# Attention feeding an activation product on one core: products of the first two slots interleaved, a bias moved ahead, and v's first load split

## The chip, the cores and the metric

The kernel runs on one core of one Trainium2 chip. The metric is the device time of one execution in microseconds; the time before the change is 308.69 us, the median of three runs (308.67 to 309.40). The profile is one execution of 308.5 us, of which the program's own instructions span 306.7 us.

## The reference

Two parts follow one another. First, attention in a sliding window of 32 to each side, for 8 batches of 8 heads with 576 positions of 64 values. Then the result of each batch, laid out as 576 rows of 512 values (4,608 rows in all), goes through two matrix products with a smoothed ReLU between them.

```python
scores = np.where(np.abs(pos[:, None] - pos[None, :]) <= 32, q @ k.T / 8, -1e9)
x = softmax(scores) @ v                 # 8 batches x 8 heads x 576 x 64 -> 4608 x 512
h = x @ w_in                            # 512 -> 2048
g = np.where(h >= 1, h, np.where(h <= -1, 0.0, (h + 1) ** 2 / 4))
out = g @ w_out                         # 2048 -> 512
```

All inputs and the output are 32-bit floats. The kernel computes in bf16 with 32-bit sums; its loads from memory convert while they run.

## The kernel before, in words

**Slots.** The second part is cut into slots. Slot `a` is block `t` of 256 rows of x (18 blocks) and piece `f` of 256 columns of w_in (8 pieces), `t, f = divmod(a, 8)`, in the loop at L482. A slot does eight TensorE products (L504: two column halves `j`, four pieces `kk` of the 512 inputs), a Relu on ScalarE (L508), and either a maximum and a product on VectorE (L515, L516) or, in the seven slots named at L379, a Square on ScalarE (L512) and one VectorE step (L513). The result stands in gT. Products with w_out follow slots later: L460 by pairs for the first two blocks (list at L378), L444 afterwards. The sum of a slot stands in one of two PSUM buffers of the pool ps_h; only slot 6 borrows one of ps_o. So slot 9 uses the buffer of slot 7, slot 10 that of slot 8.

**Attention.** It is spread among the slots by a table written out by hand (L394 to L413): scores (L227) with a band bias added by TensorE first (L206, in `add_mask`) as long as `a < 14`, Exp on ScalarE (L235), the sums with v and with ones (L293), Ln and Exp for the reciprocal (L299, L300), and a VectorE product that writes x, turned, into xT (L305). xT has four pieces `kk` of two heads each, written two at a time: one call makes pieces `y` and `y + 2`. The sums of `y = 0` fill pieces 0 and 2, those of `y = 1` pieces 1 and 3.

**The start.** Before the slots, q and k of the first half of batch 0 are turned on TensorE (L189, L187) and copied out (L190, by ScalarE and VectorE), their scores made, and the first 256 rows of x (L365 and L367, ended by L369 and L370). `keep_warm(n, ...)` puts n products of no use (L336) where TensorE would wait. Slot 1 then turns the second half of q and k (L394), and slot 2 makes the scores that need it.

**The loads.** All engines work in the order of the program (L73). GpSimd issues the loads of L85 (halves of q and k), L106 (v), L110 (w_in), L115 (w_out), L92 and L98 (q and k of later batches) in one queue. Its order at the start is: k's first half; four pieces of v for batch 0; w_in's columns 0 to 511 as four loads (256 columns, two halves of the partitions each); the second halves of q and k; w_in's columns 512 to 1023 as four loads, 1024 to 1535 as two, 1536 to 1791 as two; w_out; the last columns of w_in. Then GpSimd copies the masks (L151, L153) and goes on with w_out and the next batches. Each of these loads waits until the one issued eight before it has landed, as the semaphores of the built program show. v of a batch stands in `vn` as 18 chunks of 64 positions by two heads; chunks 0 to 8 belong to `y = 0`, 9 to 17 to `y = 1`. The first 256 rows of x need chunks 0 to 4 and 9 to 13; the sums of slot 3 need chunks 5 to 7 beside, and those of slots 4 and 5 need the rest.

Of the kernel before, what the change touches and what calls it, by code (L numbers as in the profile page):

```python
# [7 lines left out]
FP = mybir.dt.float32  # L8
# [6 lines left out]
def kernel(  # L15
# [84 lines left out]

    def load_v(b, n):
        if b not in vn:
            vn[b] = nat.tile([128, 2 * NC, 2, D], BF, name="vn", tag="vn", bufs=3)
        h, a = divmod(n, 2)
        y = NY * h + 2 * a
        nc.gpsimd.dma_start(out=vn[b][64 * a:64 * a + 64, :, h], in_=v[b, y:y + 2].rearrange("y s d -> (y s) d")  # L106
                            .rearrange("(c r) d -> r c d", r=64))

# [24 lines left out]
    for n in range(4):  # L133
        load_v(0, n)
    V.memset(ones, 1.0)
# [6 lines left out]
    def put(todo):  # L142
        for fn, *x in todo:
            fn(*x)
# [3 lines left out]
    w += [(load_w_in, c, c + 256, h) for c in range(1536, DFF, 256) for h in range(2)]  # L148
    put(w[:4] + [(load_half, 1, t, h) for t in range(2) for h in range(2)] + w[4:12])
    put([(load_w_out, 0, 0, 4)] + w[12:])  # L150
# [59 lines left out]

    def scores(b, ys, pars, cs, eng, pool=ps_s, w=128):

        if b not in pt:
            pt[b] = ptp.tile([128, 2, 2, 2, 512], BF, name="pt")
        ps = two_banks(pool)
        n = 0
        if eng is None:
            cols = (ys[1] - ys[0]) * (pars[1] - pars[0]) * (cs[1] - cs[0])
            add_mask([ps[:, h] for h in range(2)], cols, w)
# [126 lines left out]
    with tc.tile_pool(name="ps_p", bufs=1, space=bass.MemoryType.PSUM) as ps_p:  # L346
        keep_warm(11, ps_h, "hp")

        V.memset(qkT(0, 0).rearrange("d (y s) -> d y s", y=NY)[:, :, S // 2:352], 0.0)
        for b in range(LONG):  # L350
            V.memset(qkT(b, 0).rearrange("d (y s) -> d y s", y=NY)[:, :, S - PAD:], 0.0)
        V.memset(qkT(0, 1).rearrange("d (y s) -> d y s", y=NY)[:, :, S // 2:320], 0.0)
        qn[0, 0] = cast(q32, "qb", 5)
        qq = [tpose(0, n, 0, (A.copy, V.tensor_copy)[n], tp1(ps_h)) for n in range(2)]
        for x in qq:
            x()
        kk = [tpose(0, n, 1, (A.copy, V.tensor_copy)[n], tp1((ps_n, ps_p)[n])) for n in range(2)]
        keep_warm(3, ps_h, "hp")
        for x in kk:
            x()  # L360
        scores(0, (0, 1), (0, 2), (0, 2), None)
        scores(0, (0, 2), (0, 1), (2, 3), None, ps_n, 32)
        scores(0, (1, 2), (0, 2), (0, 2), None, ps_p)
        keep_warm(4, ps_h, "hp")
        e0 = sums(0, 0, 0, TB)  # L365
        keep_warm(2, ps_h, "hp")
        e1 = sums(0, 1, 0, TB, ps_p)  # L367
        keep_warm(7, ps_h, "hp")
        e0()  # L369
        e1()  # L370
# [98 lines left out]
    def run(pos):  # L469
# [9 lines left out]
        for end in todo:  # L479
            end()  # L480

    for a in range(NF * NB + NF):  # L482
        t, f = divmod(a, NF)
# [10 lines left out]
        if t < NB:  # L494
            if t not in gT:
                gT[t] = gtp.tile([128, 2 * NF, TB], BF, name="gT", tag="gT")
            r0 = TB * t % RING
            if a == 6:
                hp = ps_o.tile([128, 2, TB], FP, name="hp", tag="op")
            else:  # L500
                hp = ps_h.tile([128, 2, TB], FP, name="hp", tag="hp")
            for j in range(2):
                for n, kk in enumerate((0, 2, 1, 3)):
                    nc.tensor.matmul(hp[:, j], w_in[:, kk, 256 * f + 128 * j:256 * f + 128 * j + 128],  # L504
                                     xT[:, kk, r0:r0 + TB], start=n == 0, stop=n == 3)

# [47 lines left out]
```

The softmax here doesn't subtract the row's maximum and nothing guards it: scores larger than these inputs give would overflow.

## Time and profile before

| What | us |
|---|---|
| median of three runs | 308.69 |
| span of the profile | 306.7 |
| PE busy | 299.9 (98%) |
| VectorE busy | 242.1 (79%) |
| ScalarE busy | 192.5 (63%) |
| products of the slots, L504, 1,152 | 149.4 |
| products with w_out, L444, 496 | 126.9 |
| first product of a slot | 13.73 |

The page gives busy times for each engine: PE is TensorE's matrix work, PEld its loads of weights, DVE VectorE, ACT ScalarE, POOL GpSimd, whose issue of loads counts as its work. Where it has 40 slices, each digit is a tenth of busy time in 1/40 of the span, some 7.7 us. A line of the timeline has a start in us, a length, an engine, a line of the code and an operation, and in brackets the idle time of the engine before it with what ended it. "Landing" is the time from the issue of a load until its data is announced. A start of the chain of waits is followed by the length and the work that the end of the program was waiting for.

### The profile page before, as it was taken

What the parts mean: (1) busy time and instruction counts of PE and PEld (TensorE: products, weight loads), DVE (VectorE), ACT (ScalarE), POOL (GpSimd) and SP (SyncE); (2) the same over time, 40 slices, a digit from 0 to 9 for tenths busy, and PEclk for the clock granted to TensorE, in tenths of its full rate; (3) what the DMA queues carried; (4) which work ended last, traced back from release to release, by engine and by line L of the source; (5) the groups of instructions that cost most, each with busy time, mean ns of one, the idle gap of its engine ahead of it and who ended that gap; (6) DMA issues with size and microseconds to landing.
All of it is one profiled execution on the core that took longest, in us unless ns stands there. A gap on an engine that the chain in (4) does not pass through costs nothing.

```text
span 306.7 us, 8496 instructions
## 1 busy us (share of the span) xinstructions
PE 299.9 (98%) x3650; PEld 206.6 (67%) x3650; DVE 242.1 (79%) x376; ACT 192.5 (63%) x320; POOL 77.4 (25%) x92
## 2 busy tenths in 40 slices
PE   8989999999999999999999999999999999999995
PEld 3567878876666666666666666666666666666654
DVE  4278568888888888889888888889888888888760
ACT  3688886738856767666656666566676666554431
POOL 8799461028008106400450003700000000000000
PEclk9999999999999999999999999999999999999999
DMA  9999999999999999996899156990811010010111
GB/s 153 182 197 198 177 201 152 174 152 149 138 206 89 170 191 107 159 94 142 102 170 138 34 108 91 167 150 17 177 50 36 34 36 36 35 36 34 60 45 68
DMA packets 137173, 35.70 MB, mean 116 GB/s; under 512 B 122160, under 2 KB 132912, under 8 KB 137136
## 3 DMA queue, kind: packets, MB, share of 16 engines
q0 software_dynamic: 102976, 18.06, 83.2%
q1 hardware_dynamic: 34016, 16.81, 25.6%
q8 instruction: 28, 0.46, 0.6%
q10 hardware_dynamic: 144, 0.29, 0.3%
q14 instruction: 9, 0.07, 0.1%
HBM read 36.70 MB, written 9.44 MB: 150 GB/s over the span
## 4 chain that ended last, share of the span: by engine, by line
PE 89%; ACT 3%; DVE 2%; DMA 2%; issue 1%; POOL 1%; POOLq 0%; ACTq 0%
PE hp L504 39%; PE op L444 36%; PE bb L293 6%; PE op L460 4%; PE bb L227 2%; DMA vn<-in_v_dram 2%; PE op L433 1%; ACT pt L235 1%; POOL vn L106 1%; PE tp L187 1%; DVE xT L305 1%; ACT rc L300 1%; DVE mx L515 1%; ACT lr L299 1%; DVE gT L513 0%
## 5 line engine op out<-in xcount | busy, mean ns | idle before, releaser
L504 PE MATMUL hp<-xT,w_in 128*128 128x256 bf16 x1152 | 149.4, 273 | 1.7 <-DMA w_in<-in_moe_w_in_dram 0.8
L508 ACT ACTIVATE rr<-hp 128x512 f32<-128x512 f32 x144 | 85.7, 595 | 87.8 <-PE hp L504 87.7
L504 PEld LDWEIGHTS <-w_in 128*128 128x128 bf16 x1152 | 112.0, 98 | 41.1 <-issue 2.3
L444 PE MATMUL op<-w_out,gT 128*128 128x512 bf16 x496 | 126.9, 380 | 0.0
L515 DVE TENSOR_TENSOR mx<-hp,rr 128x512 f32<-128x512 f32 x137 | 94.5, 690 | 30.8 <-ACT rr L508 28.9
L516 DVE SCALAR_TENSOR_TENSOR gT<-rr,mx 128x512 bf16<-128x512 f32 x137 | 95.2, 695 | 4.7
L444 PEld LDWEIGHTS <-gT 128*128 128x128 bf16 x496 | 46.1, 98 | 34.8
L98 POOL DMA_DIRECT2D qn<-in_q_dram x12 | 14.6, 1221 | 111.4 <-DMA kT<-kn 107.5
L235 ACT ACTIVATE pt<-bb 128x1024 bf16<-128x1024 f32 (+1 forms) x33 | 32.7, 1002 | 5.0 <-PE bb L227 3.7
L305 DVE TENSOR_TENSOR xT<-bb,rc 128x512 bf16<-128x512 f32 (+1 forms) x32 | 21.0, 658 | 10.1 <-ACT rc L300 9.6
L106 POOL DMA_DIRECT2D vn<-in_v_dram x32 | 27.5, 891 | 4.9 <-DMA w_out<-in_moe_w_out_dram 4.2
L300 ACT ACTIVATE rc<-lr 128x512 f32<-128x512 f32 (+2 forms) x40 | 23.5, 587 | 1.3
L449 ACT COPY osb<-op 128x512 f32<-128x512 f32 x31 | 18.1, 583 | 8.7 <-PE op L444 8.3
L299 ACT ACTIVATE lr<-bb 128x512 f32<-128x512 f32 (+2 forms) x40 | 22.0, 551 | 0.4 <-PE bb L293 0.3
L201 DVE TENSOR_TENSOR pt<-pt,mask 128x1024 bf16<-128x1024 bf16 (+1 forms) x33 | 20.3, 614 | 0.5 <-ACT pt L235 0.5
L293 PE MATMUL bb<-pt,ones 64*64 64x256 bf16 (+3 forms) x352 | 19.6, 256 | 0.1
L293 PE MATMUL bb<-pt,vn 64*64 64x128 bf16 (+3 forms) x712 | 18.4, 204 | 0.1
L293 PEld LDWEIGHTS <-vn 64*64 64x64 bf16 x712 | 16.7, 107 | 0.3 <-DMA vn<-in_v_dram 0.3
L460 PE MATMUL op<-w_out,gT 128*128 128x256 bf16 x128 | 16.5, 273 | 0.0
L293 PEld LDWEIGHTS <-ones 64*64 64x64 bf16 x352 | 10.2, 105 | 8.9 <-issue 8.9
L98 POOL DMA_DIRECT2D kn<-in_k_dram x12 | 14.6, 1230 | 0.5 <-issue 0.5
L227 PE MATMUL bb<-qT,kT 64*64 64x128 bf16 (+1 forms) x520 | 13.1, 217 | 0.3 <-DVE kT L190 0.2
(59 smaller groups left out, 115.1 us busy)
## 6 DMA issues: line engine op xcount, KB each, us to landing
out_dram<-osb SPq DMA_DIRECT2D x35, 256.0 KB, 2.5
vn<-in_v_dram POOLq DMA_DIRECT2D x32, 144.0 KB, 10.2
qn<-in_q_dram POOLq DMA_DIRECT2D x12, 288.0 KB, 6.9
kn<-in_k_dram POOLq DMA_DIRECT2D x12, 288.0 KB, 8.9
w_in<-in_moe_w_in_dram POOLq DMA_DIRECT2D x12, 128.0 KB, 5.7
w_out<-in_moe_w_out_dram POOLq DMA_DIRECT2D x4, 256.0 KB, 6.6
w_out<-in_moe_w_out_dram POOLq DMA_DIRECT2D x2, 512.0 KB, 15.8
kh<-in_k_dram POOLq DMA_DIRECT2D x4, 144.0 KB, 5.1
```

Of the source, the lines that this page charges most:

```text
L98: nc.gpsimd.dma_start(out=x[:, :, h], in_=src[b, NY * h:NY * h + NY].rearrange("y s d -> (y s) d") .rearrange("(u p) d -> p u d", p=128))
L106: nc.gpsimd.dma_start(out=vn[b][64 * a:64 * a + 64, :, h], in_=v[b, y:y + 2].rearrange("y s d -> (y s) d") .rearrange("(c r) d -> r c d", ...
L235: A.activation(p, ps[:, :, :w * n].rearrange(like, y=m), AF.Exp, scale=D ** -0.5)
L293: nc.tensor.matmul(bb[HD[h], a, o + c0:o + c1], ones[HD[a]] if c is None else vn[b][HD[a], c, h], p(a, h), start=n == 0, stop=True, skip_g ...
L299: A.activation(lr[:, :, :D0], bb[:, :, D0:2 * D0], AF.Ln)
L300: A.activation(rc[:, :, :D0], lr[:, :, :D0], AF.Exp, scale=-1.0)
L444: nc.tensor.matmul(o, gT[tt // 2][:, j, 128 * (tt % 2):128 * (tt % 2) + 128], w_out[:, j], start=not done, stop=len(done) == 2 * NF - 1, s ...
L460: nc.tensor.matmul(o[:, tt], gT[p][:, j, 128 * tt:128 * tt + 128], w_out[:, j, 256 * half:256 * half + 256], start=not done, stop=len(done ...
L504: nc.tensor.matmul(hp[:, j], w_in[:, kk, 256 * f + 128 * j:256 * f + 128 * j + 128], xT[:, kk, r0:r0 + TB], start=n == 0, stop=n == 3)
L508: A.activation(rr, hp, AF.Relu, scale=0.5, bias=0.5)
L515: V.tensor_max(mx, hp, rr)
L516: V.scalar_tensor_tensor(g, rr, 1.0, mx, op0=ALU.min, op1=ALU.mult)
```

## The change

Three things are changed at the start; what is computed stays the same.

v of batch 0 is loaded in two steps: chunks 0 to 13 of its four pieces where all 18 were loaded before, and chunks 14 to 17, again as four loads, behind w_in's columns 512 to 767. This is meant to bring v's first part, and the loads behind it, in earlier.

The bias of the first scores is added ahead of k's copies instead of after them, with one product of no use in front of it for three; further fillers are fewer (three for four, none for two, six for seven). This is meant to let the first scores begin as soon as k's copies end.

The products of slots 0 and 1 are interleaved: all eight that need the first half of x (pieces 0 and 2), for both slots, and then the eight that need the second half. This is meant to use the time between the two halves of x. The order of later slots stays as it is.

```diff
-    def load_v(b, n):
+    def load_v(b, n, c0=0, c1=2 * NC):
...
-        nc.gpsimd.dma_start(out=vn[b][64 * a:64 * a + 64, :, h], in_=v[b, y:y + 2].rearrange("y s d -> (y s) d")
-                            .rearrange("(c r) d -> r c d", r=64))
+        nc.gpsimd.dma_start(out=vn[b][64 * a:64 * a + 64, c0:c1, h], in_=v[b, y:y + 2].rearrange("y s d -> (y s) d")
+                            .rearrange("(c r) d -> r c d", r=64)[:, c0:c1])
...
-        load_v(0, n)
+        load_v(0, n, 0, 14)
...
-    put(w[:4] + [(load_half, 1, t, h) for t in range(2) for h in range(2)] + w[4:12])
+    put(w[:4] + [(load_half, 1, t, h) for t in range(2) for h in range(2)]
+        + w[4:6] + [(load_v, 0, n, 14, 2 * NC) for n in range(4)] + w[6:12])
...
-    def scores(b, ys, pars, cs, eng, pool=ps_s, w=128):
+    def scores(b, ys, pars, cs, eng, pool=ps_s, w=128, ready=None):
...
-        ps = two_banks(pool)
+        ps = ready or two_banks(pool)
         n = 0
-        if eng is None:
+        if eng is None and not ready:
...
-        keep_warm(3, ps_h, "hp")
+        keep_warm(1, ps_h, "hp")
+        first = two_banks(ps_s)
+        add_mask([first[:, h] for h in range(2)], 4, 128)
         for x in kk:
             x()
-        scores(0, (0, 1), (0, 2), (0, 2), None)
+        scores(0, (0, 1), (0, 2), (0, 2), None, ready=first)
         scores(0, (0, 2), (0, 1), (2, 3), None, ps_n, 32)
         scores(0, (1, 2), (0, 2), (0, 2), None, ps_p)
-        keep_warm(4, ps_h, "hp")
+        keep_warm(3, ps_h, "hp")
         e0 = sums(0, 0, 0, TB)
-        keep_warm(2, ps_h, "hp")
         e1 = sums(0, 1, 0, TB, ps_p)
-        keep_warm(7, ps_h, "hp")
+        keep_warm(6, ps_h, "hp")
...
+    def project(hp, f, r0, todo, first, last):
+
+        for n, (j, kk) in enumerate(todo):
+            nc.tensor.matmul(hp[:, j], w_in[:, kk, 256 * f + 128 * j:256 * f + 128 * j + 128],
+                             xT[:, kk, r0:r0 + TB], start=first and n == 0, stop=last and n == len(todo) - 1,
+                             skip_group_check=True)
...
-            r0 = TB * t % RING
-            if a == 6:
-                hp = ps_o.tile([128, 2, TB], FP, name="hp", tag="op")
-            else:
-                hp = ps_h.tile([128, 2, TB], FP, name="hp", tag="hp")
-            for j in range(2):
-                for n, kk in enumerate((0, 2, 1, 3)):
-                    nc.tensor.matmul(hp[:, j], w_in[:, kk, 256 * f + 128 * j:256 * f + 128 * j + 128],
-                                     xT[:, kk, r0:r0 + TB], start=n == 0, stop=n == 3)
+            if a == 0:
+                hps = [ps_h.tile([128, 2, TB], FP, name="hp", tag="hp") for _ in range(2)]
+                for y in range(2):
+                    for f2 in range(2):
+                        project(hps[f2], f2, 0, [(j, y + 2 * m) for j in range(2) for m in range(2)], y == 0, y == 1)
+            elif a > 1:
+                pool, tag = (ps_o, "op") if a == 6 else (ps_h, "hp")
+                hps = [pool.tile([128, 2, TB], FP, name="hp", tag=tag)]
+                project(hps[0], f, TB * t % RING, [(j, kk) for j in range(2) for kk in (0, 2, 1, 3)], True, True)
+            hp = hps.pop(0)
```

## The prediction

> **What bounds the kernel now.** I read the page's busy shares first, then the chain of waits for the start, then the timeline from 16 to 33 us with all engines, then the single lines that issue transfers. The page says where time can be won at all:
>
> ```profile
> PE 299.9 (98%) x3650; PEld 206.6 (67%) x3650; DVE 242.1 (79%) x376; ACT 192.5 (63%) x320; POOL 77.4 (25%) x92
> ...
> PE   8989999999999999999999999999999999999995
> ...
> DMA  9999999999999999996899156990811010010111
> ```
>
> TensorE is full but for the first slices, so only an earlier entry into the full stretch moves the end. Asked for PE's waits between 60 and 210 us, the trace names none. The chain of waits for the start reads (start, length, what):
>
> ```profile
> 5.50 5.13 DMA vn<-in_v_dram
> ...
> 10.67 0.52 PE bb L293 x17
> ...
> 11.22 0.61 ACT lr L299
> ...
> 13.80 0.70 DVE xT L305
> ...
> 14.54 1.70 PE hp L504 x14
> ...
> 18.93 0.65 DVE kT L190
> ```
>
> v's last piece lands at 10.63, the softmax sums follow, ScalarE does Ln and Exp twice, and the second half of x is ready at 14.50. From there the chain runs through slot 1's activation and the copies of k. This is the stretch that the change shortens. What comes next decides what the end gets of it. The timeline (start, length, engine, line, operation):
>
> ```profile
> 18.02 1.03 PE L504 MATMUL hp<-xT,w_in 128*128 128x256 bf16 x8 [0.59 <-DMA w_in<-in_moe_w_in_dram]
> ...
> 20.14 1.05 PE L504 MATMUL hp<-xT,w_in 128*128 128x256 bf16 x8
> ...
> 21.43 0.62 ACT L508 ACTIVATE rr<-hp 128x512 f32<-128x512 f32 x1
> ...
> 22.39 1.03 PE L504 MATMUL hp<-xT,w_in 128*128 128x256 bf16 x8 [0.24 <-DMA w_in<-in_moe_w_in_dram]
> ...
> 28.79 1.04 PE L504 MATMUL hp<-xT,w_in 128*128 128x256 bf16 x8
> ...
> 29.86 0.60 ACT L508 ACTIVATE rr<-hp 128x512 f32<-128x512 f32 x1 [0.48 <-PE hp L504]
> 30.30 1.03 PE L504 MATMUL hp<-xT,w_in 128*128 128x256 bf16 x8 [0.47 <-DVE gT L513]
> ...
> 31.15 0.69 DVE L513 SCALAR_TENSOR_TENSOR gT<-hp,mx 128x512 bf16<-128x512 f32 x1 [0.91 <-ACT mx L512]
> ...
> 32.04 1.04 PE L504 MATMUL hp<-xT,w_in 128*128 128x256 bf16 x8
> ```
>
> These are the products of slots 2, 3, 4, 8, 9 and 10. Slots 2 and 4 already wait for w_in, slot 4 for the 512-column pair. From slot 4's start at 22.39 to slot 8's end at 29.83 PE runs without a wait. So the chain through ScalarE and VectorE that ends in the 0.47 us wait at slot 9 has a second chain beside it, almost as long: transfer of w_in, slot 4, PE full. The transfers themselves, by the views of the lines that issue them: v's first four, then the 512-column w_in pair (min/median/max of an issue in ns, first and last start):
>
> ```profile
> L106 POOL DMA_DIRECT2D vn<-in_v_dram x4: 873/879/898, 2.9 to 5.5; - x4
> ...
> DMA to landing us min/median/max: 5.1/5.3/5.5
> ```
>
> ```profile
> L110 POOL DMA_DIRECT2D w_in<-in_moe_w_in_dram x2: 620/626/632, 15.2 to 15.8; - x2
> ...
> DMA to landing us min/median/max: 5.4/5.9/6.5
> ```
>
> The second of the pair is issued at 15.77 and lands 6.5 later, at 22.26: that is slot 4's wait.
>
> **What the Trainium skill says.** "DMA: Bandwidth & Descriptors", section "Issuing engines are not separate DMA queues": all queues share 16 engines. The trace agrees: the DMA view is full in every slice from 5 to 27 us, so moving bytes within a queue moves waiting from one consumer to the next and removes none. The same page, "Anatomy of one DMA", puts about 2 us of fixed cost on a transfer. Here a transfer issued into an idle queue at 67.13 or 92.90 shows its first packets after 1.9 us, and the loads above take 4.7 to 6.5, so most of that is queueing. "TensorE: Matmul & The Clock Gate", section "The HAM clock gate", lets the clock fall after an idle window of about 3.4 us; the page shows full clock throughout, and no gap that the change opens (below) reaches 0.5 us.
>
> **The change part by part.**
>
> *v cut to 14 of 18 chunks.* Each v piece is 147,456 bytes written, and the four drop 4/18 of that: 131,072 bytes. From 5.6 to 9.6 the DMA view moves 148 GB/s, so v's last piece lands 131,072 / 148,000 = 0.89 us earlier, at 9.75. The slot 0 and 1 sums of x need chunks 0 to 4 and 9 to 13 alone. All that is queued behind v gains the same 0.89: w_in's first four, the second half of q and k, w_in's third pair (slot 2's wait ends at 17.1).
>
> *Bias earlier, fewer warm-up products.* One warm-up of 0.21 in place of three lets the bias end before k's last copy ends at 8.15; the scores start at 8.19 for 8.37, so ScalarE's three Exp run from 8.63 to 10.74 for 8.81 to 10.92. The sums of the first half need the second Exp (9.83) and v (9.75), take the 0.67 that they took without their wait, and end at 10.5, behind the third Exp. Ln starts at 10.77 for 11.22: 0.45 won. Four ScalarE steps of 0.62 and one VectorE product of 0.70 follow unchanged: x's second half at 14.05 for 14.50. The dropped warm-ups leave PE gaps of 0.3 to 0.4; cost nil, since PE waits there anyway.
>
> *Products interleaved.* Eight products on the first half of x now run before 14.05 (12.8 to 13.7; w_in's second pair must land by then: 14.28 - 0.89 = 13.4). After the second half, slot 0 needs four products and slot 1 eight, where it was six and fourteen. At 1.70/14 = 0.121 each: slot 0 is done 0.45 + 2 x 0.121 = 0.7 earlier, slot 1 0.45 + 6 x 0.121 = 1.2 earlier. ScalarE takes slot 1's Relu at 15.3 for 16.27, its Square ends at 16.6 for 17.53; VectorE, with slot 0's two steps and slot 1's in front (16.03 becomes 15.3), ends the copy of k at 18.77 for 19.57. So the scores of slot 2 start **0.8 us** earlier. The transposes in front need k's second half, 16.70 - 0.89 = 15.8, in time.
>
> *The late chunks.* They are put between w_in's third and fourth pair. Bytes in front of the fourth pair and of the 512-column pair are then the same as before: their landings gain nothing. Four more transfers cost GpSimd 4 x 0.64 (the w_in row; by the v row at most 4 x 0.88), less 4 x 0.07 by which the shorter v issues shrink (0.88 for 18 chunks, 0.64 for w_in's 4, so 0.017 a chunk): some 2.3 us later issues. Each GpSimd load also waits for the eighth before it (0.28 after its landing, as the 1.1 us wait on that line shows for the load issued at 14.56), which is now a k half landing at 15.0 or 15.8: the fourth pair is issued at 15.3 and 16.1 for 12.83 and 14.56. Behind the waiting issues stand all later loads of w_in and w_out, for which slots 3 to 9 wait. The queue's backlog hides this if the first packets follow an issue by 1.9 us, as after the idle spells: 15.3 + 1.9 = 17.2, and the packets in front end at about 17.2. If a short load needs 3.0 (the first k load's 1.26 to its landing of 5.64, less 0.7 of issue and 0.7 of packets at 198 GB/s), the queue runs dry for up to 0.55. I take nil to 0.1, and keep 0.55.
>
> *The sum.* Slot 3's fourth pair lands at 19.3 as before, about when PE now wants it (20.14 - 0.8). Slot 4 would be reached at 21.4 but its pair lands at 22.3: PE's win is gone there but for the queue's +0.1. From slot 4 PE is full to slot 8's end, 29.83 + 0.1; the VectorE chain that made slot 9 wait until 30.30 is earlier now and no longer binds. Slot 8's Relu, Square and VectorE step still follow its products, 29.86 to 31.85, and free the buffer for slot 10: 31.9 + 0.1 for 32.04. The win at the end is 0.16 - 0.1 = **0.06 to 0.16 us** of the 0.8: 308.6.
>
> **The rivals.** *Carried through, 307.7 (33%).* If the 512-column pair lands earlier too, the win passes. For it: its second load needed 1.73 after the first, where 256 KB at 198 GB/s take 1.32, so 0.4 of that landing is a disturbance that may fall elsewhere; and the short transfers may overlap with their neighbours. Then slot 4 starts up to 0.8 to 1.0 earlier: 308.69 - 1.0 = 307.7. Against it: every byte in front of the pair is still there. *Queue dry, slower, 309.6 (25%).* A window of eight loads, four of them small, holds fewer bytes: 0.55 dry, the pair at 22.9, and w_out's second piece, issued 1.4 late (GpSimd's mask copies move along), lands at 28.4 to 28.7 where slot 7 wants it at 27.92. PE loses 0.55 at slot 4 and 0.4 there: 308.69 + 0.95 = 309.6. Against it: 1.9 us twice after idle spells. *Swallowed, 308.6 (42%)* is the forecast.
>
> **How the numbers follow.** Three quarters of the first rival lie below 307.76 (0.3% faster): 0.25. Seven tenths of the second lie above 309.62: 0.18. Within 0.3%: 0.57. The range reaches from under the first rival to the second, 307.5 to 309.6.
>
> **What would show it.** After: v's last landing near 9.75, Ln at 10.8, x's second half at 14.05, k's copy at 18.8; then slot 4's products waiting about 1 us for w_in and starting at 22.3 to 22.5, and slot 10's at about 31.9. The forecast is wrong if slot 4 starts before 22 (carried through), or if slot 3 or slot 7's w_out product waits long for its load (queue dry).

## The result, and the profile after

The changed kernel takes 312.72 us, the median of six runs (312.17 to 314.91), where the kernel before took 308.68 (six runs, 308.50 to 309.40). The ratio is 1.0142, with a 95% interval of 1.0108 to 1.0177: 4.0 us slower, outside the range that the prediction gave. A second comparison, with six more runs, gave 312.54 against 308.58, a ratio of 1.0136 (1.0114 to 1.0159). Ratios leave out runs over 1.5% above the fastest of the same kernel; these are one run of the kernel before, 440.26 us at a mean clock of 0.657, and one of the 17 runs of an experiment below, 314.18 us at 0.987.

The profiled execution spans 310.5 us, 3.8 more than before. The page of the changed kernel, its busy shares, three of its 40-slice rows and the group of the slots' products:

```profile
PE 294.3 (95%) x3607; PEld 206.9 (67%) x3644; DVE 241.8 (78%) x376; ACT 192.8 (62%) x320; POOL 79.5 (26%) x96
...
PE   7868999999999999999999999999999999999995
...
PEclk9997999999999999999999999999999999999999
...
GB/s 152 185 136 192 195 193 160 161 192 107 171 171 100 172 145 119 167 125 112 112 158 139 36 110 113 139 160 35 149 77 36 34 36 36 35 36 34 50 53 68
...
L487 PE MATMUL hp<-xT,w_in 128*128 128x256 bf16 x1152 | 150.6, 274 | 4.2 <-DMA w_in<-in_moe_w_in_dram 3.0
```

Two things are new. In the products' group, the waits that w_in's loads end sum to 3.0 us; they were 0.8 before. And the fourth digit of the clock is a 7: before, all were 9. All of it lies before 31 us; from slice 5 on, PE is as full as it was. The fall of PE's busy time from 299.9 is in part not real: 37 records of products are missing from this trace (3,607 for 3,644 weight loads), 35 of them in the w_out products of L446.

The timeline of PE in the changed kernel shows where it lies (start, length, engine, line, operation, and the idle time before it with what ended it):

```profile
17.97 1.03 PE L487 MATMUL hp<-xT,w_in 128*128 128x256 bf16 x8 [0.66 <-DVE gT L523]
...
20.64 1.03 PE L487 MATMUL hp<-xT,w_in 128*128 128x256 bf16 x8 [0.89 <-DMA w_in<-in_moe_w_in_dram]
...
24.75 1.70 PE L487 MATMUL hp<-xT,w_in 128*128 128x256 bf16 x8 [2.10 <-DMA w_in<-in_moe_w_in_dram]
...
27.30 1.56 PE L487 MATMUL hp<-xT,w_in 128*128 128x256 bf16 x8
...
34.06 1.03 PE L487 MATMUL hp<-xT,w_in 128*128 128x256 bf16 x8 [0.33 <-DVE gT L523]
...
35.81 1.03 PE L487 MATMUL hp<-xT,w_in 128*128 128x256 bf16 x8
```

These are slots 2, 3, 4, 5, 9 and 10. Slot 3 waits 0.89 us for w_in's fourth pair, slot 4 waits 2.10 for the 512-column pair. Slot 4 starts at 24.75 where it started at 22.39: 2.36 us later. Its eight products then take 1.70 in place of 1.03, slot 5's 1.56. Slot 10 starts at 35.81 for 32.04, 3.77 us later, and that is the whole difference of the spans (3.8). So the loss has two parts, **2.36 us at slot 4** and, since slot 9 waits 0.14 less than before, 3.77 - 2.36 + 0.14 = **1.55 us between slots 4 and 9**. The second part is the clock. The same trace cut into windows (from:to, length, then busy time and count of PE, PEld, DVE, ACT and POOL, the granted clock, the DMA share, and GB/s):

```profile
24.50:25.00 0.50, 0.25 (x3) 0.25 (x4) 0.50 (x1) 0.00 (x0) 0.50 (x2) 0.96 1.43 192
25.00:26.00 1.00, 1.00 (x7) 0.71 (x5) 0.01 (x1) 0.00 (x0) 1.00 (x2) 0.50 1.45 196
...
28.00:28.50 0.50, 0.50 (x5) 0.37 (x4) 0.50 (x1) 0.47 (x2) 0.50 (x1) 0.63 1.45 197
```

TensorE runs at half clock from about 24.96 (0.96 of the first window is 0.04 us at half) to about 28.37 (0.63 of the last is 0.37 us): 3.41 us, in which half of the work, 1.7 us, is lost. That is about the second part.

**What slot 4 waited for.** The chain of waits of the changed kernel's start (start, length, work):

```profile
6.10 2.36 POOL w_in L110 x4
8.47 6.03 DMA qh<-in_q_dram
...
14.78 1.22 POOL vn L106 x2
...
16.06 0.61 POOL w_in L110
...
16.86 1.22 POOL w_in L110 x2
18.08 0.04 issue
18.11 6.50 DMA w_in<-in_moe_w_in_dram
24.61 0.14 issue
24.75 1.70 PE hp L487 x8
```

Before, this chain ran over v, ScalarE and the products of slots 0 and 1. Now it runs through GpSimd's queue: a load of q that lands at 14.49, the third late piece of v that waited for its place, three w_in loads one after the other, and the transfer of the second half of the 512-column pair, issued at 18.11 for 15.77 and landing at 24.61 for 22.26. From issue to landing it took 6.50 us, as before (6.49), so here the delay could be put down to the issue alone. The run with the split alone (below) speaks against that: there the same load was issued 1.53 us later than before and took 7.32, and landed at 24.62. The windows show what happened to the transfers meanwhile. Before:

```profile
16.00:18.00 2.00, 1.44 (x39) 1.12 (x37) 1.82 (x3) 1.70 (x3) 2.00 (x4) 1.00 1.45 194
18.00:20.00 2.00, 1.75 (x38) 1.19 (x40) 1.84 (x4) 1.42 (x3) 1.90 (x4) 1.00 1.27 202
20.00:22.00 2.00, 2.00 (x72) 1.56 (x60) 1.55 (x2) 1.91 (x5) 2.00 (x3) 1.00 1.35 199
22.00:24.00 2.00, 1.76 (x53) 1.31 (x42) 1.38 (x2) 1.97 (x5) 2.00 (x3) 1.00 1.45 192
```

After:

```profile
16.00:18.00 2.00, 1.03 (x29) 0.73 (x24) 1.97 (x4) 1.97 (x4) 1.75 (x3) 1.00 1.34 114
18.00:20.00 2.00, 1.75 (x40) 1.21 (x40) 1.45 (x3) 1.22 (x3) 1.96 (x5) 1.00 1.10 125
20.00:22.00 2.00, 1.36 (x24) 1.01 (x28) 1.05 (x2) 1.33 (x4) 1.96 (x4) 1.00 1.10 148
22.00:24.00 2.00, 0.65 (x48) 0.51 (x36) 1.47 (x2) 1.97 (x4) 1.94 (x3) 1.00 1.21 157
```

The last column falls from 192 to 202 GB/s to 114 to 157 for 8 us. In these 8 us the queue moved 2 x (114 + 125 + 148 + 157) = 1,088 KB for 2 x (194 + 202 + 199 + 192) = 1,574 KB; the 486 KB that are missing are 2.5 us of transfer at 197 GB/s. That is slot 4's 2.36. The page's DMA row of tenths is full in both kernels and shows none of this: it says that the engines had a transfer, not how fast they moved it. The GB/s row does show it: its third slice is 136, and was 197 before.

### The profile page after: what moved, and what is told of

Its sections match the earlier page's. It is cut to its first block, busy times and chain, and to the rows that moved or that the text cites. A ratio compares the mean times of both kernels' runs of the same rounds, so it can differ in the third digit from the quotient of the medians.

```text
span 310.5 us, 8452 instructions
## 1 busy us (share of the span) xinstructions
PE 294.3 (95%) x3607; PEld 206.9 (67%) x3644; DVE 241.8 (78%) x376; ACT 192.8 (62%) x320; POOL 79.5 (26%) x96
## 4 chain that ended last, share of the span: by engine, by line
PE 88%; DMA 4%; POOL 3%; issue 2%; ACT 1%; DVE 0%; POOLq 0%; ACTq 0%
PE hp L487 39%; PE op L446 34%; PE bb L294 6%; PE op L462 4%; DMA w_in<-in_moe_w_in_dram 2%; PE bb L228 2%; DMA qh<-in_q_dram 2%; POOL vn L106 1%; POOL w_in L110 1%; PE op L435 1%; PE tp L188 1%; ACT pt L236 1%; POOL kh L85 0%; DVE gT L523 0%; ACT mx L522 0%
## 5 line engine op out<-in xcount | busy, mean ns | idle before, releaser
L446 PE MATMUL op<-w_out,gT 128*128 128x512 bf16 x461 | 119.6, 379 | 5.0 <-issue 4.8
L446 PEld LDWEIGHTS <-gT 128*128 128x128 bf16 x496 | 46.1, 98 | 34.8
L106 POOL DMA_DIRECT2D vn<-in_v_dram x36 | 29.7, 860 | 4.8 <-DMA w_out<-in_moe_w_out_dram 3.3
```

What stands on the lines that cost most here:

```text
L106: nc.gpsimd.dma_start(out=vn[b][64 * a:64 * a + 64, c0:c1, h], in_=v[b, y:y + 2].rearrange("y s d -> (y s) d") .rearrange("(c r) d -> r c ...
L446: nc.tensor.matmul(o, gT[tt // 2][:, j, 128 * (tt % 2):128 * (tt % 2) + 128], w_out[:, j], start=not done, stop=len(done) == 2 * NF - 1, s ...
```

## The experiments

The runs come in four groups, each beside runs of the kernel before: its median was 308.82 us beside the first four, then 308.79, 308.72 and 308.58. The theory that the expectations call Q is this. GpSimd's queue holds eight loads, since each waits for the landing of the one eight before it. A late load of v (chunks 14 to 17 of one piece, 32 KB) takes one of these eight places, and an issue of 0.61 us, as long as a load of w_in does, but brings a quarter of its bytes. With four of them in the queue there are too few bytes under way to keep the 16 DMA engines at their rate, and everything behind them comes later. The rivals are stated with each run. Where the expectations below say that "the fourth pair" lands at 22 us or later, the 512-column pair is meant; the fourth pair itself landed at 19.25 before and at 20.51 after.

### Which of the changes costs the time

The changed kernel with v's loads whole; the bias and the interleaved products stay:

```diff
-        load_v(0, n, 0, 14)
+        load_v(0, n)
...
-        + w[4:6] + [(load_v, 0, n, 14, 2 * NC) for n in range(4)] + w[6:12])
+        + w[4:12])
```

> The changed kernel with v's first load whole again (no late chunks): the early bias, the fewer fillers and the interleaved products stay. Theory Q (the four late loads hold back w_in, and the idle wait at slot 4 halves TensorE's clock): the loss goes; 308.3 to 308.7, the 512-column pair of w_in lands at 22.3, clock 1.00. Theory F (the dropped fillers or the new order of the products let the clock fall): the loss stays, over 311, with a stretch at half clock.

And the reverse, the kernel before with only the loads changed:

```diff
-        load_v(0, n)
+        load_v(0, n, 0, 14)
...
-    put(w[:4] + [(load_half, 1, t, h) for t in range(2) for h in range(2)] + w[4:12])
+    put(w[:4] + [(load_half, 1, t, h) for t in range(2) for h in range(2)]
+        + w[4:6] + [(load_v, 0, n, 14, 2 * NC) for n in range(4)] + w[6:12])
```

> The kernel before with v's load split alone, the late chunks behind w_in's third pair; bias, fillers and products as before. Theory Q: all of the loss is here, 312 to 313, the 512-column pair lands at about 24.6 and slot 4 waits for it by about 2 us. Theory F: 308.7, as before.

Without the split: 308.65 us, ratio 0.9993 (0.9979 to 1.0007). The bias and the interleaving alone move nothing that can be measured. The trace of that run holds a warning: its loads are those of the kernel before, yet the pair landed at 23.09 and slot 4 started at 23.23, both 0.8 us later than before (that execution took 309.22 us). So two single traces can differ by that much without any cause in the loads, and where a smaller difference matters the medians have to decide.

With the split alone: 310.91 us, the median of four runs, ratio 1.0109 (1.0054 to 1.0165). That is less than the 312 to 313 that was expected. In its trace (timeline of PE; here the products stand at L505) slot 4 reads

```profile
24.76 1.03 PE L505 MATMUL hp<-xT,w_in 128*128 128x256 bf16 x8 [2.54 <-DMA w_in<-in_moe_w_in_dram]
```

The same start as in the changed kernel, 24.76 for 24.75, at full clock. So the split of the loads alone makes the delay. In this execution the clock stayed whole (1.03 for the eight products); one of its four runs, 314.19 us, shows a mean clock of 0.987. The half clock is thus something that the gap can bring, not something that the split always brings.

### Is the half clock a cost of its own?

Ten products of no use in front of slot 4 of the changed kernel, so that PE is not idle there:

```diff
                 pool, tag = (ps_o, "op") if a == 6 else (ps_h, "hp")
+                if a == 4:
+                    keep_warm(10, ps_o, "op")
                 hps = [pool.tile([128, 2, TB], FP, name="hp", tag=tag)]
```

> The changed kernel with ten products of no use (0.21 each) in front of slot 4's products, into a free buffer of ps_o, in the time in which TensorE waits for w_in. If the half clock after that wait is a cost of its own: 1.5 us less, 311.2, clock 1.00, the pair still at 24.6. If the wait for w_in alone sets the time: no change, 312.7.

It took 311.21 us (four runs), ratio 1.0087 (1.0069 to 1.0104): 1.5 less than the changed kernel. Since the two came from different groups of runs, both were run again beside one another:

> The changed kernel itself once more, beside the one with fillers on the same chip, for how its runs divide between the later load and the half clock. If the half clock is a part of the loss that comes and goes, the runs with a mean clock of 0.995 or less (one window of 3.4 us at half clock is 0.0055 of the span) are about 1.5 us longer than those at 0.998 to 1.000, which are at 310.5 to 311.5. Rival: the runs at full clock are as long as the others (312 and more), so that the clock explains the one traced run only and the loads' own delay varies.

> The changed kernel with ten products of no use in front of slot 4, once more, beside the changed kernel on the same chip. If the half clock is a part of the loss, none of its runs shows 0.995 or less and its median is 1.0 to 1.6 us below that of the changed kernel, at 310.7 to 311.5. Rival: the two medians agree within 0.5 us.

The changed kernel: 312.54 us, and all six runs show a mean clock of 0.987 to 0.995 (one stretch of 3.41 us at half clock is 3.41 / 2 / 310.5 = 0.0055). With fillers: 311.76 us, five runs, clocks 0.998 to 1.000, ratio 1.0102 (1.0090 to 1.0114). The gain is 0.8: neither the 1.0 to 1.6 that was expected nor the rival's 0.5 or less. None of these six runs of the changed kernel kept the full clock, so they can't be set against one another by clock, as the expectation meant to. In the profiled execution with fillers the pair landed still later, at 25.86 for 25.01 in the changed kernel beside it: the timeline of PE shows the fillers, a wait all the same, and slot 4 at full clock.

```profile
22.53 2.33 PE L337 MATMUL z<-warm 128*128 128x512 bf16 x9
...
26.00 1.03 PE L487 MATMUL hp<-xT,w_in 128*128 128x256 bf16 x8 [1.14 <-DMA w_in<-in_moe_w_in_dram]
```

In the changed kernel's second trace slot 4 starts at 25.14 and slot 10 at 36.14, 11.00 later; here slot 10 starts at 35.51, 9.51 after slot 4. The difference, 1.49, is the half clock, and the later landing took 0.85 of it back. The clock is thus a cost of its own, 1.49 us between these two traces and 0.8 or 1.5 by the medians, beside a delay of the load that varies between executions. It isn't in every run: of the first six of the changed kernel two show a clock of 1.000, and they took 312.17 and 314.05, so there something else cost as much, a still later load perhaps. No trace of such a run exists, and that stays open.

### Does it help to put the late loads further back?

```diff
-        + w[4:6] + [(load_v, 0, n, 14, 2 * NC) for n in range(4)] + w[6:12])
+        + w[4:10] + [(load_v, 0, n, 14, 2 * NC) for n in range(4)] + w[10:12])
```

> The changed kernel with the four late chunk loads one place later, behind the fourth pair and the 512-column pair. Theory Q, places in the window of eight: what was behind the late loads is now in front and gains from v's shorter first load; the pair lands at 21.4 to 22, slot 4 starts earlier than before, time 307.9 to 308.6. If four more loads cost 2 us to whatever stands near them wherever they are put: w_in's columns 1536 on or the sums of slot 4 wait for them instead, over 310.

310.50 us (four runs), ratio 1.0056 (1.0041 to 1.0071): not the 307.9 to 308.6 of theory Q, but the other case that the expectation names. The timeline of PE, slots 4 and 7 and the w_out products after slot 7:

```profile
21.69 1.03 PE L487 MATMUL hp<-xT,w_in 128*128 128x256 bf16 x8 [0.57 <-DMA w_in<-in_moe_w_in_dram]
...
28.22 1.03 PE L487 MATMUL hp<-xT,w_in 128*128 128x256 bf16 x8 [1.50 <-DMA w_in<-in_moe_w_in_dram]
29.67 1.03 PE L462 MATMUL op<-w_out,gT 128*128 128x256 bf16 x8 [0.42 <-DMA w_out<-in_moe_w_out_dram]
```

Slot 4 comes 0.70 us earlier than before the change in this trace: that would be the gain that the change was made for. But w_in's last columns land at 28.09 for 26.33, and PE pays 1.50 at slot 7 and 0.42 more behind it. The cost moved to what stands behind the four small loads.

### Half as many late loads, and loads with hardly any bytes

Only the last two of v's four loads split, at the place that the change chose:

```diff
-        load_v(0, n, 0, 14)
+        load_v(0, n, 0, 2 * NC if n < 2 else 14)
...
-        + w[4:6] + [(load_v, 0, n, 14, 2 * NC) for n in range(4)] + w[6:12])
+        + w[4:6] + [(load_v, 0, n, 14, 2 * NC) for n in (2, 3)] + w[6:12])
```

> The changed kernel with two late loads in place of four: the chunks of the first two loads of v are whole again, only those of the last two are split, and their late loads stand at the same place, behind w_in's third pair. Theory Q (each late load takes a place among the eight loads under way and an issue of GpSimd for bytes worth only 0.2 us, so each costs what stands behind it about 0.5 us): half the loss, the fourth pair lands at about 23.3 to 23.7 us for 24.6, slot 4 waits about 1.0 us, no half clock, 309.3 to 310.2 us. Rival (the loss comes of splitting at all, whatever the number: the queue runs dry once and stays slow): the pair still lands after 24.3 and the time is 311 or more.

The kernel before with four tiny loads added. v is whole, nothing is left out, and nobody reads what they bring:

```diff
+    def dummy(n):
+        z = early.tile([64, 1, D], BF, name=f"dummy{n}")
+        nc.gpsimd.dma_start(out=z, in_=v[0, n].rearrange("(c r) d -> r c d", r=64)[:, 0:1])
...
-    put(w[:4] + [(load_half, 1, t, h) for t in range(2) for h in range(2)] + w[4:12])
+    put(w[:4] + [(load_half, 1, t, h) for t in range(2) for h in range(2)]
+        + w[4:6] + [(dummy, n) for n in range(4)] + w[6:12])
```

> The kernel before with four tiny loads added behind w_in's third pair, 64 partitions of 64 values each, into a tile that nobody reads; nothing of v is split and nothing else is changed. Theory Q (places and issues, not bytes): the fourth pair lands at 24.0 us or later for 22.3, slot 4 waits 2 us or more, 310.3 to 311.5 us. Rival (it is the bytes of the late chunks and their packets that delay the pair): the dummies carry almost none, so the pair lands at 22.3 to 22.6 and the time stays at 308.6 to 309.0.

And the same number of tiny transfers, but from SyncE's queue, at the same time:

```diff
         if a == 0 or a > 3:
             flush()
+        if a == 0:
+            for n in range(4):
+                z = early.tile([64, D], BF, name=f"dummy{n}")
+                nc.sync.dma_start(out=z, in_=xT[0:64, 0, 64 * n:64 * n + 64])
```

> The kernel before with four tiny copies added (64 partitions of 64 values each, from x into a tile that nobody reads), as in the run with dummies, but issued by SyncE's queue once x is written at about 14 us, so that they take no place among GpSimd's eight loads and none of its issue time; the 16 DMA engines carry them all the same. Theory Q (the loss comes of places and issues in GpSimd's queue): no loss, the fourth pair lands at 22.0 to 22.8 us and 308.5 to 309.0 us. Rival (small transfers among the large ones slow the DMA engines): the pair lands at 23.3 or later, as with GpSimd's dummies, and 310 us or more.

Two late loads: 309.70 us, 17 runs from 308.09 to 314.18, ratio 1.0033 (1.0012 to 1.0054). The pair lands at 23.36 and slot 4 starts 1.1 us later than before, half of the 2.36; but that trace alone can't be told from the 23.09 of the run with v's loads whole. By the medians half of the late loads cost 0.9 us of the 4.0. Of the 17 runs four show a clock of 0.995 or less, where none was expected; they are the four that took 311.44 and more.

Tiny loads in GpSimd's queue: 312.83 us (five runs, 310.32 to 314.42), ratio 1.0125 (1.0102 to 1.0149), as bad as the change itself and worse than the 311.5 expected at most, though they bring 32 KB in all. The traced execution is the longest of the five. The windows and the timeline of PE of that run (products at L509):

```profile
16.00:18.00 2.00, 1.49 (x38) 1.11 (x36) 1.85 (x3) 1.81 (x4) 1.63 (x4) 1.00 0.86 95
18.00:20.00 2.00, 1.61 (x40) 1.32 (x40) 1.45 (x3) 1.24 (x3) 1.94 (x4) 1.00 1.10 125
20.00:22.00 2.00, 0.15 (x12) 0.01 (x4) 1.38 (x2) 1.50 (x4) 2.00 (x4) 1.00 1.05 117
22.00:24.00 2.00, 1.41 (x28) 1.06 (x32) 0.00 (x0) 0.34 (x1) 1.90 (x4) 1.00 0.97 117
```

```profile
22.59 1.03 PE L509 MATMUL hp<-xT,w_in 128*128 128x256 bf16 x8 [2.44 <-DMA w_in<-in_moe_w_in_dram]
...
26.37 1.86 PE L509 MATMUL hp<-xT,w_in 128*128 128x256 bf16 x8 [1.38 <-DMA w_in<-in_moe_w_in_dram]
```

The rate falls to 95, then stays at 117 to 125 GB/s; slots 3 and 4 wait 2.44 and 1.38 us, the pair lands at 26.23, and the clock is half from 24.04 to 30.87. So neither the bytes of the late loads nor v's being split is needed for the loss. The tiny loads consist of 128-byte packets, as those of v do, so this run doesn't part small loads from small packets.

The tiny transfers from SyncE's queue: 308.44 us, ratio 0.9988 (0.9978 to 0.9997); the pair lands at 22.07. The view of the added copies, which run at the time at which the others ran (issues from 13.5 to 15.4):

```profile
L497 SPq DMA_DIRECT2D dummy<-xT x4: 514/593/597, 13.5 to 15.4; - x4
...
DMA to landing us min/median/max: 4.6/4.7/5.0
```

They too consist of 128-byte packets, the page counts them on the same 16 engines, and they cost nothing. What costs, then, is small loads in GpSimd's queue, where each takes a place and an issue. Two rivals stay: the copies from SyncE's queue come from on-chip memory and convert nothing, so this run doesn't exclude that small loads from memory cost something wherever they are issued. And the place isn't parted from the issue. In the changed kernel's trace both bind in turn: up to 18.11 us GpSimd waits several times for a landing (0.44 and 0.75 us in front of late loads), and from 18.72 to 21.93 it issues load after load without a pause, each time with the eighth load before it landed 0.67 us or more earlier.

### A larger number of large loads, and places given back

The kernel before with the 512-column pair of w_in as four loads of 256 columns, two loads more with the same bytes:

```diff
-    w += [(load_w_in, 1024, 1536, h) for h in range(2)]
+    w += [(load_w_in, c, c + 256, h) for c in range(1024, 1536, 256) for h in range(2)]
...
-    put(w[:4] + [(load_half, 1, t, h) for t in range(2) for h in range(2)] + w[4:12])
-    put([(load_w_out, 0, 0, 4)] + w[12:])
+    put(w[:4] + [(load_half, 1, t, h) for t in range(2) for h in range(2)] + w[4:14])
+    put([(load_w_out, 0, 0, 4)] + w[14:])
```

> The kernel before with the 512-column pair of w_in (columns 1024 to 1535) as four loads of 256 columns: two loads more, the same bytes, none of them small. Theory Q: a load of 128 KB brings as much time of transfer as it takes of issue, so nothing is lost: 308.5 to 309.0 us. Rival (every load more costs about 0.5 us to what stands behind it, whatever its size): w_in's last columns and w_out land about 1 us later, and the time is 309.4 to 310.

308.82 us, ratio 1.0002 (0.9989 to 1.0014). By the medians, two loads more cost nothing when each carries as much time of transfer as its issue takes: 128 KB at 197 GB/s are 0.66 us, an issue is 0.61. The interval leaves room for 0.4 us either way, and the trace has a small loss: w_out's second piece landed at 28.54 for 27.65, PE waited 0.46 for it, and slot 10 started at 32.56 for 32.04. Some 0.4 of the later landing had come about before the added loads.

The changed kernel with two late loads behind the 512-column pair, and w_in's last 512 columns in two loads in place of four, so that the number of loads is that of the kernel before:

```diff
-        load_v(0, n, 0, 14)
+        load_v(0, n, 0, 2 * NC if n < 2 else 14)
...
-    w += [(load_w_in, c, c + 256, h) for c in range(1536, DFF, 256) for h in range(2)]
+    w += [(load_w_in, 1536, DFF, h) for h in range(2)]
...
-        + w[4:6] + [(load_v, 0, n, 14, 2 * NC) for n in range(4)] + w[6:12])
+        + w[4:10] + [(load_v, 0, n, 14, 2 * NC) for n in (2, 3)] + w[10:12])
```

> Interleave and bias as changed; two late loads (the last two of v) behind the fourth pair and the 512-column pair, and w_in's columns 1536 to 2047 in two loads of 512 columns in place of four of 256, so that the number of loads is that of the kernel before. Theory Q: the places that the late loads take are given back by the larger loads, so the fourth pair lands at about 21.8, slot 4 starts at about 22, the last columns of w_in arrive by 26.6 and 307.9 to 308.5 us, no slower than before. Rival (a small load anywhere leaves the queue slow for microseconds after it): slot 7 waits over 1 us and the time is 309.5 or more.

308.49 us, ratio 0.9991 (0.9976 to 1.0007): the loss is gone, and no gain over the kernel before can be told. The windows give 196, 203, 173 and 198 GB/s from 16 to 24 us. Slot 4 starts at 21.88, half a microsecond before the 22.39 of the kernel before; but then slot 6 waits 0.37 for w_in, the w_out products behind it 0.27 and slot 9 0.33 for VectorE, and slot 10 starts at 32.24 for 32.04. So even with the price taken away, no gain of the start is seen at the end. The run changes three things at once (two late loads for four, their place, and w_in's last columns merged), and two late loads behind the pair without the merging were not tried; that the places given back made the difference is argued, not shown.

### Is it the large packets that stay slow?

From 20 us on all four late loads have landed, and yet the changed kernel's queue moves 148 and 157 GB/s. The changed kernel with the 512-column pair as four loads (it halves the pair's packets, from 1,024 to 512 bytes):

```diff
-    w += [(load_w_in, 1024, 1536, h) for h in range(2)]
+    w += [(load_w_in, c, c + 256, h) for c in range(1024, 1536, 256) for h in range(2)]
...
-        + w[4:6] + [(load_v, 0, n, 14, 2 * NC) for n in range(4)] + w[6:12])
+        + w[4:6] + [(load_v, 0, n, 14, 2 * NC) for n in range(4)] + w[6:14])
```

> The changed kernel with w_in's columns 1024 to 1535 in four loads of 256 columns in place of two of 512: packets of 512 bytes in place of 1,024, and two loads more. It asks why the queue stays at 125 to 157 GB/s after the late chunks. Theory Q as it stands (too few bytes under way behind the late loads, whatever the packets): slots 4 and 5 still wait about as long, the columns 1024 to 1279 land at 23.0 to 24.5 us in place of 24.6, 311 to 313 us. Rival (it is the large packets that are slow in a queue that has run dry): the rate is back at 185 GB/s or more from 20 us on, slot 4 starts by 23.2, and 309 to 310 us.

311.02 us, ratio 1.0059 (1.0039 to 1.0079). Slot 4 needs only the first 256 of these columns now; they landed at 22.65, earlier than theory Q had it, and slot 4 starts at 22.79, as its rival had it. The time and the rate decide against the rival: the windows still give 141 and 149 GB/s from 16 to 20 us, and then:

```profile
20.00:22.00 2.00, 1.88 (x56) 1.37 (x54) 0.96 (x2) 1.70 (x5) 2.00 (x4) 1.00 1.14 125
22.00:24.00 2.00, 1.22 (x24) 0.96 (x28) 1.40 (x3) 1.70 (x4) 1.30 (x4) 1.00 0.94 115
```

PE pays at slots 3, 4, 5 and 7 and at two groups of w_out products. That the pair's packets have 1,024 bytes isn't the cause.

### The bytes under way

What a stretch of the queue had under way can be worked out from the issue and the landing of each load in the traces: the loads of GpSimd's queue whose issue has ended and which have not yet landed, averaged over the stretch, and their bytes.

| | before | after | tiny loads, GpSimd | tiny copies, SyncE | pair as four |
|---|---|---|---|---|---|
| loads under way, 16 to 18 us | 6.4 | 6.7 | 6.7 | 6.5 | 6.6 |
| KB under way, 16 to 18 us | 1,053 | 480 | 407 | 1,059 | 852 |
| GB/s, 16 to 18 us | 194 | 114 | 95 | 195 | 193 |
| KB under way, 18 to 20 us | 1,183 | 699 | 573 | 1,201 | 845 |
| GB/s, 18 to 20 us | 202 | 125 | 125 | 205 | 193 |
| KB under way, 20 to 22 us | 1,093 | 1,012 | 998 | 1,124 | 965 |
| GB/s, 20 to 22 us | 199 | 148 | 117 | 195 | 197 |

From 16 to 18 us the number of loads under way is the same everywhere; their bytes are not. (From 18 to 20 us the number falls too, to 4.5 in the changed kernel and 4.7 with tiny loads for 6.4 before.) The bytes under way are the rate times the time to landing, so the rows don't prove a cause by themselves; the cause rests on the runs with tiny loads. Nor is there one amount of bytes that the queue needs. In the pair as four, 850 KB went with 193 GB/s; but from 18 to 20 us the run with two late loads had 938 KB under way and moved 143 GB/s, the split alone 889 KB and 143, while the run with the late loads behind the pair moved 198 with 780 KB.

So theory Q fits the stretch from 16 to 18 us, and not what follows: in the changed kernel the bytes are back at 1,000 KB from 20 us and the rate only at 24 us (193 GB/s). Of the 486 KB that are missing, 314 fall before 20 us and 172 after. The packet records of the traces narrow the later part. From 18 to 24 us most packets of GpSimd's queue took what they took before, 0.06 us for 512 bytes and 0.10 for 1,024, but 59 of 1,158 took over 0.18 us, up to 0.78, and these fill a fifth of the 16 engines' time; before the change it was one of 1,779. With tiny loads such packets fill 28% of that stretch, the longest with 1.7 us. What holds these packets stays open.

## Why the prediction was wrong, point by point

**What bounds the kernel.** Right as far as it went: two chains at the start, and the one over w_in and slot 4 decides what the end gets. It decided more than was thought.

**v cut to 14 chunks.** v's last landing was put at 9.75 and came at 9.87. "All that is queued behind v gains the same 0.89" failed: q's second half landed at 14.49 for 14.53, k's second at 16.57 for 16.70. In the trace, q's first packets come 0.73 earlier than before, but of the 16 parts of its landing, which the trace reports one by one, twelve were in by 12.87 and the last at 14.49. A landing is the end of the slowest part, and an earlier start needn't bring an earlier landing. In another execution it did: with the split alone the same two landed at 13.66 and 15.72, the 0.9 earlier that was forecast. Slot 4 started at 24.76 all the same, so this step isn't the one that failed.

**Bias earlier.** The scores were put at 8.19 and started at 8.80, since k's second load landed at 7.17 for 6.56, by the last of its 16 parts (fifteen were in by 6.45); Ln came at 11.25, not 10.77, and x's second half at 14.54, not 14.05. The 0.45 us weren't won in this execution. Without the split they weren't either (x's second half at 14.85), and yet the median of that run is no longer than before (308.65): the step has no weight at the end that can be measured.

**Products interleaved.** Here the mechanism shows: k's last copy ended at 19.11 for 19.57 and the scores of slot 2 started at 19.17 for 19.62, 0.45 earlier where 0.8 was put, the rest being the missing gain of the bias. All of it is gone at slot 3, which starts at 20.64 for 20.14.

**The late loads: the step that failed.** The text worked out that each load waits for the eighth before it, that the fourth pair would be issued at 15.3 and 16.1 (it was 16.06 and 16.86, for q and k landed late), and that the first packets would follow 1.9 us later, when the packets in front end. They did so, even sooner: some 1.3 us after the issue of 16.06. From there it said that "the queue's backlog hides this", took "nil to 0.1", and kept 0.55 as the most. (Its own numbers give more: with first packets after 3.0 us the queue would be empty for 15.3 + 3.0 - 17.2 = 1.1.) The pair landed 2.35 us later. So the term that it put at nil to 0.1 is the one that failed, and the error is in the question: it asked for how long the queue would be empty, and took it to move at its full rate otherwise. The queue moved 114 and 125 GB/s without being empty. "Anatomy of one DMA", of the page "DMA: Bandwidth & Descriptors" in the Trainium skill, which the prediction quoted, puts about 2 us of fixed cost on every transfer, whatever its size. It follows that a load of few bytes holds a place for at least that long. The trace agrees, with a larger number. The view of the late loads in the changed kernel:

```profile
L106 POOL DMA_DIRECT2D vn<-in_v_dram x4: 610/610/617, 12.7 to 15.4; - x4
...
DMA to landing us min/median/max: 3.4/4.3/5.3
```

Issues of 0.61 us, and 3.4 to 5.3 us in a place, for 32 KB; the four landed 0.20 to 0.25 us apart. Four of eight places and 2.4 us of GpSimd's issues carried 128 KB in the time in which they would have carried 512. Of the 2.35, 1.26 had come about by the landing of the fourth pair (20.51 for 19.25), 1.09 during the 512-column pair's own transfer.

**The clock.** "No gap that the change opens (below) reaches 0.5 us" was worked out for the bias and the fillers alone; the wait for the pair wasn't among the gaps. It was 2.10 us and brought the half clock, 1.55 us of the 3.8. "TensorE: Matmul & The Clock Gate", section "The HAM clock gate", gives a window of about 3.4 us that runs freely. The trace agrees with the length, 3.41 us. But the window ahead of it, from 21.55 to 24.96, was not idle: PE worked in it for some 1.3 us, by the windows. An idle gap of 2.1 us was enough, and ten of the changed kernel's twelve runs show the loss in their mean clock. The traces together say when a gap is enough. Within each, the changes of the clock lie whole multiples of 3.41 us apart. Cut into steps of that length from there, all 14 traces agree: the clock fell from full to half behind every step with 1.45 us or less of PE work (1.31 and 1.06 in the two traces of the changed kernel, 1.45 with tiny loads), and behind none with 1.52 or more, by the products that the traces hold. Once half, it stayed half behind a step with 2.03 us, with tiny loads. The gap of 2.54 us with the split alone lay across the end of a step, at 23.92, which left 1.71 and 2.58 us of work in the two.

**The rivals.** *Queue dry* had the cause and one of its two places: slot 4 waited, slot 7 did not. It was sized at 0.95 us because it counted the dry spell alone; the split alone cost 2.1 (310.91 for 308.82), and the whole change with the clock 4.0. *Carried through* did not come: the pair landed later. Where it landed 0.5 earlier, with two late loads behind it, slot 10 started no earlier. *Swallowed* fits the bias and the interleaving taken alone, 308.65, within the interval of that run.

**The signs.** The last sentence named the right one: slot 3 waited 0.89 us for its load. The sign that it gave for its own forecast, a start of slot 4 at 22.3 to 22.5, did not come.

## What to carry to other kernels

In a queue that allows a fixed number of loads at a time, a split load is paid by the number of loads, not by their bytes: four loads of 8 KB cost here as much as four of 32 KB. Compare the issue time of each added load with the time of its bytes (by the medians, loads with 0.66 us of bytes for 0.61 of issue were free), and count on what stands behind small loads coming later. Merging loads elsewhere, so that their number stays the same, went with no loss in one run. Before pricing an early piece, find what the end gets of it: here bias and interleaving were worth 0.45 us at slot 2 in the changed kernel's trace, and nothing in the time. And price each new wait of TensorE twice, once as idle time and once for the clock that may halve after it (about 1.5 us here).

## What had not been expected of the hardware

Four loads of 8 KB or of 32 KB in GpSimd's queue, ahead of the 512-column pair, made it land 2.35 to 3.97 us later in six traces, while as many small on-chip copies from SyncE's queue, at the same time, did nothing (308.44 us).

After the small loads the queue stayed at 115 to 157 GB/s from 20 to 24 us, with 1,000 KB under way, while a few packets of usual size (59 of 1,158 in the changed kernel from 18 to 24 us) took up to 0.78 us in place of 0.06 to 0.10. With the pair in packets of 512 bytes it was as slow, at 790 to 950 KB.

TensorE's clock halved after a 3.41 us step in which it was busy for 1.45 us or less, and kept its full speed after steps with 1.52 us and more. The longer gap of 2.54 us with the split alone did no harm because it lay across two steps; so with the gap in the same place it depends on the execution.
